# Negative score maxima as matrix rows: a DVE block transpose and eight small transfers in the windows with filler

## The chip, the core and the metric

The kernel runs on one core of a Trainium2 chip. TensorE (PE) multiplies, VectorE (DVE), ScalarE (ACT) and GpSimd (POOL) do the rest, and SyncE (SP) mostly issues DMA transfers. Matmul results land in PSUM, which is used here as eight banks of 128 x 512 floats; all other tiles are in SBUF. The metric is the device time of one execution, in microseconds, as the median of several runs.

## What is computed

A transformer block with adaptive layer norms for 2048 tokens of width 512: 32 attention heads of size 16, then a gated feed-forward layer of width 1792.

```python
mod = (silu(c) @ w_mod).reshape(1, 6, 1, -1)       # sa, ca, ga, sb, cb, gb
h = layernorm(x) * (1 + ca) + sa
q, k, v = split(h @ wqkv)                          # 32 heads of 16
p = softmax(einsum("bhqd,bhkd->bhqk", q, k) * 16 ** -0.5)
x = x + ga * (merge(einsum("bhqk,bhkd->bhqd", p, v)) @ wo)
h = layernorm(x) * (1 + cb) + sb
x = x + gb * ((silu(h @ w_gate) * (h @ w_up)) @ w_down)
```

The softmax needs the maximum of each row of scores, for each head and each query. This change concerns the way in which the negative of that maximum gets into the score matmul.

## The kernel before

All large products are made of float32r matmuls; most operands are split into a high and a low part, and three products of parts are summed.

**Units.** Attention is cut into 32 units (`NU`): a chunk of 512 queries (`ci`, four of them) times a group of four heads (`g`, eight of them). A unit has 16 steps, one for each tile of 128 keys, and each step has four *pairs*, one for each head. A pair (`pair_of`) issues one score matmul for the current step (`score`, L506) with its exponential on ACT (L508), and one matmul of queries by keys for the maxima of a unit that is to come (`max_one`, L479), whose result DVE reduces to one column (L481). The maxima run 20 steps ahead of the scores. The probabilities are multiplied with the values in half-steps (`pv_step`, L521).

**Maxima as rows.** The score matmul has keys on the PSUM partitions and queries along the free axis, so a query's maximum can't be subtracted by a per-partition bias. The operands `qop` (queries) and `kop` (keys) carry two rows more than the 48 of the products: `kop` has ones there, and rows 48 and 49 of `qop` (`KR` = 48; the same at partitions 112 and 113 for the other heads) hold the high and the low part of the negative maximum. The maxima are made with queries on the partitions, so they have to be turned.

**`max_rows(u)`** does that, when the last maximum of a unit has been issued. DVE reduces the four partial maxima to `m`, 128 queries by 16 columns (L486). Five entries are put in the list `side`, from which each following pair takes one: after two empty ones ACT makes `nm`, the negative rounded to float32r (L498) at the third pair, then comes another empty one, and at the fifth pair `rows`: PE multiplies `nm` by the identity (L491), and `m` and `nm` by the negative identity into the same PSUM bank (L492, L493), which gives the high part and the remainder as 16 rows of 256; ACT copies them to `mr` (L495); two transfers on SP's queue put each part into its rows of `qop` (L497). The bank is taken from the turn `bank`, which the score matmuls use too.

**Windows.** The order of all of this is written out by hand. `plain(steps)` runs pairs and half-steps of values alone, with scores on three PSUM banks and maxima on four. `filled(places, work)` runs a window of two steps, eight pairs, and puts between them matmuls of the other layers for an earlier chunk, the *filler* (output projection, gate-up and down products, L719); `places` says how many pieces follow each pair. In such a window scores use two banks (`Turn(4, 5)`), maxima three, and the filler has two of its own. At its end, results of the filler are worked up (`hook`) and up to six half-steps of values run. `end_steps` calls `after(i)` when four pairs are done, and `after` calls `max_rows` in one step of each unit. A gate-up job takes two windows, a down job one. Once the last maxima have been issued, only scores and filler remain in a window, with other places and banks (`ALONE`).

**Queues.** Each engine runs its instructions in the order in which they were issued, and SP's queue too: besides the rows it carries the loads of weights for the filler (`load_gu` at L652, `load_wd` at L657), the softmax denominators (L532, L537, L542) and one half of the loads of `kop` and `qop` (L404). The other half of those loads is on POOL's queue.

Of the kernel before, what the change touches and what calls it, by code (L numbers as in the profile page):

```python
# [9 lines left out]
F32 = mybir.dt.float32  # L10
F32R = mybir.dt.float32r
# [3 lines left out]
ALU = mybir.AluOpType  # L15
AX = mybir.AxisListType
# [3 lines left out]
P = 128  # L20
# [18 lines left out]
KR = 48  # L39
# [62 lines left out]
def block_kernel(ctx, tc, x, wqkv, wo, w_gate, w_up, w_down, c, w_mod, out):  # L102
    nc = tc.nc
# [18 lines left out]
    four, bank, single = Turn(0, 1, 2, 3), Turn(4, 5, 6), Turn(7)  # L122
# [326 lines left out]
    pb = ctx.enter_context(tc.tile_pool(name="pb", bufs=2, reuse_waits="tile"))  # L449
    kop[1] = pb.tile([P, 2, S], F32R, name="kop1", bufs=1)  # L450
    pf = None
    qop, mx, pts, pv, o_, due, res = {}, {}, {}, {}, {}, {}, {}
# [30 lines left out]
    def max_rows(u):  # L483

        m = pb.tile([P, 16], F32, name="m", tag="m")
        nc.vector.tensor_reduce(m, mx.pop(u).rearrange("p b s t f -> p (b s t) f"), op=ALU.max, axis=AX.X)  # L486
        nm = pb.tile([P, 16], F32R, name="nm", tag="nm")

        def rows():
            pr = bank("pr")[0:16, 0:2 * P]  # L490
            nc.tensor.matmul(pr[:, 0:P], nm.bitcast(F32), ident, start=True, stop=True)  # L491
            nc.tensor.matmul(pr[:, P:2 * P], m, minus, start=True, stop=False)  # L492
            nc.tensor.matmul(pr[:, P:2 * P], nm.bitcast(F32), minus, start=False, stop=True)  # L493
            mr = pb.tile([16, 2, P], F32R, name="mr", tag="mr", bufs=1)
            nc.scalar.copy(mr, pr.rearrange("p (r q) -> p r q", r=2))  # L495
            for r in range(2):
                nc.sync.dma_start(qop[u][KR + r:KR + r + 65:64].bitcast(F32), mr[:, r, :].bitcast(F32))  # L497
        side.extend([lambda: None, lambda: None, lambda: nc.scalar.mul(nm, m, -1.0), lambda: None, rows])  # L498

    def score(i, h):  # L500
        u, kt = divmod(i, 16)
        rows = slice(64 * (h % 2), 64 * (h % 2) + KR + 2)
        p_ = pb.tile([P, CW], F32, name="pt_", tag="pt", bufs=PTS)
        pts.setdefault(i, {})[h] = p_
        sp = bank("st_")
        nc.tensor.matmul(sp, kop[u % 3][rows, h // 2, kt * P:(kt + 1) * P], qop[u][rows, h // 2, :],  # L506
                         start=True, stop=True)
        nc.scalar.activation(p_, sp, AF.Exp, scale=SCALE)  # L508
# [51 lines left out]
    def tile_gu():  # L560
        return pf.tile([P, 4, NK, P], F32R, name="wgu", tag="wgu", bufs=2)
# [4 lines left out]
    def tile_mid():  # L566
        return pf.tile([P, 2, CW], F32R, name="mid", tag="mid", bufs=3)
# [4 lines left out]
    def as_wo(w):  # L572
        return w.rearrange("p (b k) x c -> p b k (x c)", b=2)

    def split_weights():

        def raw(src, k):
            t = tile_mid().bitcast(F32)
            nc.gpsimd.dma_start(t.rearrange("p e c -> p (e c)").rearrange("p (k c) -> p k c", k=k), src)
            return t  # L580

        def parts(hi, lo, t):
            nc.gpsimd.tensor_copy(hi, t)
            nc.gpsimd.tensor_sub(lo, t, hi.bitcast(F32))

        def store(dst, w):
            nc.gpsimd.dma_start(dst, w.bitcast(F32))

        def cols(m):
            return slice(m * FG * P, (m + 1) * FG * P)  # L590

        srcs = [(wod[:, 2 * k:2 * k + 2, :], 2) for k in range(NK // 2)]
        for m in range(NF // FG):
            srcs += [(wgd[:, :, cols(m)], NK), (wud[:, :, cols(m)], NK), (wdd[:, m * FG:(m + 1) * FG, :], FG)]
        ahead = [raw(*srcs.pop(0)) for _ in range(2)]
        yield

        def following():
            if srcs:
                ahead.append(raw(*srcs.pop(0)))  # L600
            return ahead.pop(0)

        for k in range(NK // 2):
            t = following()
            nc.gpsimd.tensor_mul(t, t, ga_bc[:, None, :].to_broadcast([P, 2, D]))
            w = tile_gu()
            parts(as_wo(w)[:, 0], as_wo(w)[:, 1], t)
            store(wo_dr[k], as_wo(w))
            yield
        for m in range(NF // FG):  # L610
            ws = [tile_gu() for _ in range(FG)]
            for e in range(2):
                t = following()
                src = t.rearrange("p e c -> p (e c)").rearrange("p (k f c) -> p f k c", k=NK, f=FG)
                for f in range(FG):
                    parts(ws[f][:, 2 * e], ws[f][:, 2 * e + 1], src[:, f])
                    if e:
                        store(gu_dr[m * FG + f], ws[f])
                yield
            t = following()  # L620
            nc.gpsimd.tensor_mul(t, t, gb_bc[:, None, :].to_broadcast([P, FG, D]))
            w = tile_wd()
            parts(w[:, 0], w[:, 1], t)
            store(wd_dr[m], w)
            yield

    class Chunk:
# [42 lines left out]
        def rows(self, t):  # L670
            return self.nt[t // 2][:, t % 2, :]
# [139 lines left out]
    side = []  # L811
# [53 lines left out]
    at(UG - 2, lambda: chunks[0].load_wo())  # L865

    weights2 = split_weights()

    def after(i):
        nonlocal pf  # L870
        for f in due.pop(i, []):
            f()
        j = i + LEAD
        if j % 16 == 15 and j < n:
            max_rows(j // 16)
        if i == -2:
            run(late)
            sm.finish()
            es_a0.close()
            pf = ctx.enter_context(tc.tile_pool(name="pf", bufs=1, side="right", reuse_waits="tile"))  # L880
            kop[2] = pf.tile([P, 2, S], F32R, name="kop2")
            ones_rows(2)
            load_k(2)
            load_q(2)
        if 0 <= i < UG and i % 16 in (3, 5, 8):
            next(weights2, None)
# [48 lines left out]

    def plain(steps, tails=()):

        nonlocal four, bank
        assert steps % WIN == 0 and done % 4 == 0
        four, bank = Turn(0, 1, 2, 3), Turn(4, 5, 6)  # L940
        for w in range(4 * steps // WIN):
            for _ in range(WIN):
                pair_of()
            if w >= 4 * steps // WIN - len(tails):
                tails[w - 4 * steps // WIN](four())
            pvs((HALVES[(w - 2) % 4] if done > 8 else 0) + (w == 4 * steps // WIN - 1), True)
            end_steps()

    def filled(places, work):

        nonlocal four, bank
        four, bank = three, Turn(4, 5)
        if done >= 4 * n - 4 * (LEAD - 1):
            places, bank = ALONE.get(places, places), Turn(4, 5, 0, 1, 5, 0, 4, 1)
        for r in range(len(places)):
            pair_of()
            take(work, places[r])
            if r % 4 == 3:
                end_steps()
        hook()  # L960
        pvs(6, False)
# [105 lines left out]
```

## Time and profile before

| what | value |
|---|---|
| median of 3 runs | 1880.32 us (1879.69 to 1880.54) |
| span of the profiled execution, first to last instruction | 1875.6 us |
| mean granted TensorE clock in it | 0.999 |
| POOL busy | 415.3 us |
| TensorE weight loads, beside the matmuls | 1160.4 us |
| L506 score matmuls, mean of one | 427 ns, 2048 of them |
| L481 reductions of maxima on DVE, mean of one | 682 ns, 2048 of them |
| L497 transfers of rows, each | 8.0 KB, 64 of them |

The span is the time from the first to the last instruction of the profiled execution; the time of a run also holds what lies before and after them. A row of a group gives the line in the code, the engine, the operation, the result and its operands with their shapes, the count, then busy time and the mean of one, and behind the second bar the time for which the engine stood idle just before such instructions, with what ended it. A row of the timeline gives start, length, engine and line, and in brackets the idle time before it. Matmuls overlap in time, so their lengths add up to more than the engine's busy time.

### The profile page before, as it was taken

Reading aid. Unit: us, or ns where it says so; the run is one execution under the profiler, and the core shown is the slowest. Engines: PE = TensorE matmul, PEld = TensorE weight load, DVE = VectorE, ACT = ScalarE, POOL = GpSimd, SP = SyncE. Lnnn points to the kernel's source line nnn. Section 1 sums busy time; section 2 is a strip of 40 time slices with the busy share of each in tenths; the row PEclk is TensorE's granted clock in tenths of the full one; section 3 lists DMA queues with packets and bytes.
Section 4 is the critical chain, followed back from the end, with each engine's and each line's share of the span. In section 5 each row is a group of like instructions: output and inputs, shape, how many; then the busy total and the mean of one; then the engine's idle time right before and its main releaser. Section 6 shows DMA issues by size and latency. Waiting matters only on the chain.

```text
span 1875.6 us, 41002 instructions
## 1 busy us (share of the span) xinstructions
PE 1846.7 (98%) x16996; PEld 1160.4 (62%) x16996; DVE 1541.8 (82%) x2558; ACT 1252.4 (67%) x2406; POOL 415.3 (22%) x498
## 2 busy tenths in 40 slices
PE   7999999999999999999999999999999999999999
PEld 5766444444455766666555667666554566667887
DVE  5548999999999888888999888889999988831643
ACT  4221888888887766777777776677878877674211
POOL 3000454456323211111133111111123011030200
PEclk9999999999999999999999999999999999999999
DMA  8855677766843534554454454453643446243642
GB/s 286 292 198 142 174 183 178 201 167 190 211 86 78 145 102 124 144 124 90 107 124 116 108 127 131 121 122 78 159 86 56 108 92 156 86 159 119 249 180 110
DMA packets 78854, 267.62 MB, mean 143 GB/s; under 512 B 17364, under 2 KB 22484, under 8 KB 57988
## 3 DMA queue, kind: packets, MB, share of 16 engines
q1 hardware_dynamic: 59820, 180.10, 33.0%
q0 software_dynamic: 18160, 84.10, 19.0%
q8 instruction: 133, 2.18, 0.5%
q10 hardware_dynamic: 688, 0.80, 0.1%
q14 instruction: 53, 0.43, 0.1%
HBM read 201.85 MB, written 62.13 MB: 141 GB/s over the span
## 4 chain that ended last, share of the span: by engine, by line
PE 95%; DVE 2%; ACT 2%; DMA 0%; issue 0%; SPq 0%; ACTq 0%; DVEq 0%
PE bank L521 26%; PE bank L506 22%; PE bank L719 19%; PE bank L479 10%; PE bank L729 7%; PE bank L209 7%; DVE mx L481 1%; PE bank L762 1%; PE bank L491 1%; PE bank L162 0%; PE bank L703 0%; DMA wm_ab<-in_w_mod 0%; DVE stt L745 0%; PE bank L279 0%; PE bank L493 0%; PE bank L492 0%
## 5 line engine op out<-in xcount | busy, mean ns | idle before, releaser
L481 DVE TENSOR_REDUCE mx<-bank 128x1 f32<-128x512 f32 x2048 | 1286.5, 682 | 119.5 <-PE bank L479 72.4
L479 PE MATMUL bank<-kop,qop 48*128 48x512 f32 x2048 | 748.0, 432 | 3.6 <-DVE mx L481 3.4
L506 PE MATMUL bank<-qop,kop 50*128 50x512 f32 x2048 | 742.1, 427 | 4.6 <-ACT pt__20499 L508 0.5
L506 PEld LDWEIGHTS bank<-qop,kop 50*128 50x128 f32 x2048 | 347.0, 184 | 305.6 <-issue 63.3
L479 PEld LDWEIGHTS bank<-kop,qop 48*128 48x128 f32 x2048 | 343.9, 184 | 30.7 <-DVE mx L481 14.4
L719 PE MATMUL bank<-act,wgu 64*128 64x512 f32 x1872 | 297.9, 392 | 0.0
L719 PEld LDWEIGHTS bank<-act,wgu 64*128 64x128 f32 x1872 | 188.4, 187 | 30.9 <-DVE m L779 0.3
L548 POOL TENSOR_TENSOR on<-o,rb 128x512 f32<-128x512 f32 x31 | 39.7, 1282 | 442.9 <-DMA rb<-d_dr 304.0
L719 PE MATMUL bank<-wd,mid 64*128 64x512 f32 x912 | 136.5, 397 | 0.0
L781 POOL CAST mid<-m 128x512 fp32r<-128x512 f32 x40 | 24.3, 609 | 430.1 <-PE bank L479 165.5
L719 PEld LDWEIGHTS bank<-wd,mid 64*128 64x128 f32 x912 | 93.3, 185 | 12.0 <-issue 0.8
L209 PE MATMUL bank<-hT,wqs 128*128 128x512 f32 x384 | 95.7, 399 | 2.1 <-DVE prt L369 0.8
L209 PEld LDWEIGHTS bank<-hT,wqs 128*128 128x128 f32 x384 | 70.3, 188 | 24.3 <-issue 6.1
L777 DVE SCALAR_TENSOR_TENSOR q<-th,bank 128x512 f32<-128x512 f32 x56 | 37.7, 673 | 57.4 <-ACT th L773 57.2
L773 ACT ACTIVATE th<-bank 128x512 f32<-128x512 f32 x56 | 33.2, 593 | 58.3 <-PE bank L729 57.9
L793 DVE TENSOR_TENSOR x<-bank,x 128x512 f32<-128x512 f32 x84 | 53.8, 684 | 20.4 <-PE bank L506 20.2
L369 DVE TENSOR_TENSOR prt<-bank,prt 128x512 fp32r<-128x512 f32 x32 | 22.0, 688 | 46.5 <-ACT prt L367 46.5
L367 ACT CAST prt<-bank 128x512 fp32r<-128x512 f32 x32 | 18.8, 587 | 60.2 <-PE bank L209 46.9
L779 DVE TENSOR_TENSOR m<-bank,q 128x512 f32<-128x512 f32 x56 | 38.7, 691 | 21.2 <-PE bank L729 19.1
L729 PE MATMUL bank<-wd,mid 128*128 128x512 f32 x216 | 52.1, 394 | 0.4 <-DVE mid L782 0.3
L782 POOL TENSOR_TENSOR mid<-m,mid 128x512 fp32r<-128x512 f32 x40 | 51.6, 1291 | 3.3
L719 PE MATMUL bank<-wgu,act 64*128 64x512 f32 x288 | 47.7, 394 | 0.1
(6282 smaller groups left out, 5155.0 us busy)
## 6 DMA issues: line engine op xcount, KB each, us to landing
wgu<-gu_dr SPq DMA_DIRECT2D x48, 1024.0 KB
wd<-wd_dr SPq DMA_DIRECT2D x28, 1024.0 KB
kop<-kd SPq DMA_DIRECT2D x33, 768.0 KB
kop<-kd POOLq DMA_DIRECT2D x29, 768.0 KB, 8.5
gu_dr<-wgu POOLq DMA_DIRECT2D x14, 1024.0 KB, 14.1
kd<-prt SPq DMA_DIRECT2D x16, 512.0 KB
qd<-prt SPq DMA_DIRECT2D x16, 512.0 KB
kop<-gu_dr SPq DMA_DIRECT2D x8, 1024.0 KB
```

The costliest lines, as they stand in the source:

```text
L209: nc.tensor.matmul(pt, lhs(a, k), rhs(b, k), start=(n == 0), stop=(n == 3 * nk - 1))
L479: nc.tensor.matmul(pm, qop[u][rows, s, qt * P:(qt + 1) * P], kop[u % 3][rows, s, kc * CW:(kc + 1) * CW], start=True, stop=True)
L481: nc.vector.tensor_reduce(mx[u][:, b, s, qt, kc:kc + 1], pm, op=ALU.max, axis=AX.X)
L506: nc.tensor.matmul(sp, kop[u % 3][rows, h // 2, kt * P:(kt + 1) * P], qop[u][rows, h // 2, :], start=True, stop=True)
L521: nc.tensor.matmul(pv[u][32 * h:32 * h + 32, cols], v_flat[:, e0:e0 + 32], p_[h][:, cols], start=(kt == 0 and half == 0), stop=(kt == 15), ...
L548: mul.tensor_mul(on, o, rb)
L719: nc.tensor.matmul(outs[e], lhs(e, a, k)[rows], rhs(b, k)[rows], start=(ph == 0 and j == 0), stop=(j == z and (ph == 1 or trade is not None)),
L729: nc.tensor.matmul(outs[e], lhs(e, a, k), rhs(b, k), start=(j == 0), stop=(j == z))
L777: nc.vector.scalar_tensor_tensor(q, th, 1.0, outs[0], op0=ALU.add, op1=ALU.mult)
L779: nc.vector.tensor_mul(m32, outs[1], q)
L782: (nc.gpsimd if slow else nc.vector).tensor_sub(mid[:, 1, :], m32, mid[:, 0, :].bitcast(F32))
L793: nc.vector.tensor_add(ch.x2[:, t, :], outs[e], ch.x2[:, t, :])
```

## The change

`max_turned(u)` is added beside `max_rows(u)`, and a flag `beside` chooses between them: `filled` sets it and `plain` clears it. In `max_turned` the tile `parts` holds, for each of 128 queries, 16 high parts and 16 low parts. At the second following pair ACT writes the high parts; at the fourth DVE writes the low parts (`m` times -1, less the high part) and transposes `parts` in four blocks of 32 x 32 into `turned`; at the fifth eight transfers on SP's queue bring the rows of the blocks to `qop`, 16 partitions by 32 floats each, one for each part and each block of 32 queries. The three PE products with the identities, the PSUM bank and the ACT copy are not issued in these units.

```diff
--- before.py
+++ after.py
@@ -497,6 +497,26 @@
                 nc.sync.dma_start(qop[u][KR + r:KR + r + 65:64].bitcast(F32), mr[:, r, :].bitcast(F32))
         side.extend([lambda: None, lambda: None, lambda: nc.scalar.mul(nm, m, -1.0), lambda: None, rows])
 
+    def max_turned(u):
+
+        m = pb.tile([P, 16], F32, name="m", tag="m")
+        nc.vector.tensor_reduce(m, mx.pop(u).rearrange("p b s t f -> p (b s t) f"), op=ALU.max, axis=AX.X)
+        parts = pb.tile([P, 2, 16], F32R, name="parts", tag="parts", bufs=1)
+        turned = pb.tile([P, 32], F32, name="turned", tag="turned", bufs=1)
+
+        def blocks():
+            nc.vector.scalar_tensor_tensor(parts[:, 1], m, -1.0, parts[:, 0].bitcast(F32), op0=ALU.mult,
+                                           op1=ALU.subtract)
+            nc.vector.transpose(turned, parts.rearrange("p r j -> p (r j)").bitcast(F32))
+
+        def rows():
+            for r in range(2):
+                for p in range(4):
+                    dst = qop[u][KR + r:KR + r + 65:64].bitcast(F32).rearrange("b s (t q) -> b (s t) q", t=4)
+                    j = 32 * p + 16 * r
+                    nc.sync.dma_start(dst[:, :, 32 * p:32 * p + 32], turned[j:j + 16])
+        side.extend([lambda: None, lambda: nc.scalar.mul(parts[:, 0], m, -1.0), lambda: None, blocks, rows])
+
     def score(i, h):
         u, kt = divmod(i, 16)
         rows = slice(64 * (h % 2), 64 * (h % 2) + KR + 2)
@@ -865,6 +885,7 @@
     at(UG - 2, lambda: chunks[0].load_wo())
 
     weights2 = split_weights()
+    beside = False
 
     def after(i):
         nonlocal pf
@@ -872,7 +893,7 @@
             f()
         j = i + LEAD
         if j % 16 == 15 and j < n:
-            max_rows(j // 16)
+            (max_turned if beside else max_rows)(j // 16)
         if i == -2:
             run(late)
             sm.finish()
@@ -935,7 +956,8 @@
 
     def plain(steps, tails=()):
 
-        nonlocal four, bank
+        nonlocal four, bank, beside
+        beside = False
         assert steps % WIN == 0 and done % 4 == 0
         four, bank = Turn(0, 1, 2, 3), Turn(4, 5, 6)
         for w in range(4 * steps // WIN):
@@ -948,7 +970,8 @@
 
     def filled(places, work):
 
-        nonlocal four, bank
+        nonlocal four, bank, beside
+        beside = True
         four, bank = three, Turn(4, 5)
         if done >= 4 * n - 4 * (LEAD - 1):
             places, bank = ALONE.get(places, places), Turn(4, 5, 0, 1, 5, 0, 4, 1)
```

## The prediction

> **What bounds the kernel now.** I read the page first (busy time, chain of waits, costliest groups), then the order of time around one of the places that the change touches.
>
> ```profile
> span 1875.6 us, 41002 instructions
> ...
> PE 1846.7 (98%) x16996; PEld 1160.4 (62%) x16996; DVE 1541.8 (82%) x2558; ACT 1252.4 (67%) x2406; POOL 415.3 (22%) x498
> ...
> PE 95%; DVE 2%; ACT 2%; DMA 0%; issue 0%; SPq 0%; ACTq 0%; DVEq 0%
> ...
> L479 PE MATMUL bank<-kop,qop 48*128 48x512 f32 x2048 | 748.0, 432 | 3.6 <-DVE mx L481 3.4
> L506 PE MATMUL bank<-qop,kop 50*128 50x512 f32 x2048 | 742.1, 427 | 4.6 <-ACT pt__20499 L508 0.5
> ```
>
> PE is busy 98% of the span and makes up 95% of the chain that ended last. Over the whole run it stood idle 3.6 us before the maximum matmuls (L479) and 4.6 us before the score matmuls (L506). So work taken off PE should come off the end, as long as nothing new holds PE up.
>
> The change acts only where the flag `beside` is set as a unit's maxima fall due: counting windows in `plain` and `filled` by the constants, that is in 15 of 32 units (11 to 16, 19 to 24, 29 to 31). Unit 11 in order of time on PE (start, length, what):
>
> ```profile
> 629.43 0.50 PE L506 MATMUL bank<-qop,kop 50*128 50x512 f32 x1
> 629.43 0.50 PE L479 MATMUL bank<-kop,qop 48*128 48x512 f32 x1
> 629.86 0.39 PE L491 MATMUL bank<-ident,nm 128*16 128x128 f32 x2
> 630.09 0.38 PE L492 MATMUL bank<-minus,m 128*16 128x128 f32 x2
> 630.31 0.38 PE L493 MATMUL bank<-minus,nm 128*16 128x128 f32 x2
> 630.62 0.49 PE L506 MATMUL bank<-qop,kop 50*128 50x512 f32 x1
> 630.62 0.50 PE L479 MATMUL bank<-kop,qop 48*128 48x512 f32 x1
> ```
>
> The three turning matmuls stand in PE's line from 629.86 to 630.62, 0.76 us in which no score or filler runs.
>
> **The change part by part.**
>
> *Removed from PE.* The bare price is 15 x 0.76 = 11.4 us. A better yardstick is in the trace itself: a window of `filled` (two steps, eight pairs, filler, six value half-steps) that holds a turn, beside one of the same kind that holds none. Each row runs from the start of a window's first score matmul to that of the next window; the second column is its length, then busy time by engine.
>
> ```profile
> 629.43:637.13 7.70, 7.70 (x83) 5.21 (x80) 6.31 (x10) 5.53 (x10) 0.00 (x0) 1.00 0.12 28
> 1598.06:1605.76 7.70, 7.70 (x83) 5.19 (x80) 6.33 (x10) 5.53 (x10) 0.00 (x0) 1.00 0.12 26
> 671.31:678.09 6.78, 6.78 (x78) 4.61 (x74) 6.13 (x10) 5.06 (x9) 1.89 (x2) 1.00 0.28 82
> 643.90:650.76 6.86, 6.86 (x76) 4.64 (x73) 6.20 (x10) 5.55 (x10) 0.00 (x0) 1.00 1.00 140
> 740.42:748.30 7.88, 7.88 (x82) 5.39 (x79) 6.63 (x11) 5.10 (x11) 0.00 (x0) 1.00 0.18 35
> 1542.47:1550.34 7.87, 7.87 (x84) 5.35 (x80) 6.65 (x11) 5.12 (x11) 0.00 (x0) 1.00 0.17 36
> 657.60:664.53 6.93, 6.93 (x76) 4.78 (x72) 6.34 (x11) 4.65 (x10) 0.00 (x0) 1.00 0.17 35
> 699.41:706.43 7.02, 7.02 (x76) 4.80 (x72) 6.42 (x11) 5.11 (x11) 0.00 (x0) 1.00 1.01 145
> 901.06:909.30 8.24, 7.85 (x83) 5.19 (x80) 6.55 (x12) 5.04 (x12) 1.08 (x2) 1.00 0.16 65
> 1314.03:1322.29 8.26, 7.87 (x82) 5.20 (x78) 6.58 (x12) 5.03 (x12) 1.08 (x2) 1.00 0.17 67
> 1653.34:1660.63 7.29, 7.24 (x74) 4.55 (x71) 1.22 (x2) 5.31 (x10) 0.00 (x0) 1.00 0.04 15
> 1674.10:1679.94 5.84, 5.84 (x68) 4.21 (x65) 0.00 (x0) 4.35 (x8) 0.00 (x0) 1.00 0.81 331
> ```
>
> Gate-up windows: rows 1 and 2 are the first and last of nine with a turn, 7.70; rows 3 and 4 have none, 6.78 and 6.86, mean 6.82. Difference 0.88, times nine 7.9 us. Down windows: rows 5 and 6 are the first and last of three with a turn, 7.875 on the mean; rows 7 and 8 without, mean 6.975; 0.90 times three, 2.7 us. Units 16 and 24 (rows 9 and 10, 8.25) sit in the last down window of a chunk, where PE also stood 0.39 us (8.24 less 7.85 busy) in front of the turn for a PSUM bank; 8.25 less 6.975 is 1.275, twice 2.55 us. Unit 31 (row 11) falls where no maxima are left: 7.29 against 5.84 of the next kind, 1.45 us. Sum 14.6 us. It already holds the turn's slot in the rotation of two banks, and that the pair after it could not follow the pair before it directly.
>
> *Removed from ACT.* One copy of 16x256 per unit. ACT is not on the chain in these windows (5.5 of 7.7 us busy), so this counts for nothing by itself.
>
> *Moved on ACT.* The multiplication by -1 is issued one pair earlier. It must still end before DVE reaches the new subtraction, and the maxima `m` must be there when ACT gets to it. DVE (first and third fence line) and ACT (second) around unit 11 and, last two, unit 13:
>
> ```profile
> 625.99 2.53 DVE L481 TENSOR_REDUCE mx<-bank 128x1 f32<-128x512 f32 x4
> ...
> 627.69 0.21 ACT L498 ACTIVATE nm<-m 128x16 fp32r<-128x16 f32 x1
> ...
> 630.00 0.69 DVE L481 TENSOR_REDUCE mx<-bank 128x1 f32<-128x512 f32 x1 [1.49 <-PE bank L506]
> ...
> 739.50 1.27 DVE L481 TENSOR_REDUCE mx<-bank 128x1 f32<-128x512 f32 x2
> 741.00 0.69 DVE L481 TENSOR_REDUCE mx<-bank 128x1 f32<-128x512 f32 x1 [0.22 <-PE bank L506]
> ```
>
> `m` is made just ahead of the four reductions that begin at 625.99; an activation of one pair earlier than 627.69 finds it done. On DVE the subtraction comes behind those four, at 628.52; even at its old place the product is ready at 627.90. Neither engine waits.
>
> *Added to DVE.* Two small operations, a subtraction of 128x16 and a transpose of 128x32. The trace has no transpose. Nearest rows:
>
> ```profile
> L684 DVE SCALAR_TENSOR_TENSOR rs<-rs,rs x3: 161/161/163, 1742.1 to 1743.3; 128x4 f32<-128x4 f32 x3
> ...
> L486 DVE TENSOR_REDUCE m<-mx x32: 200/220/221, 176.8 to 1650.0; 128x16 f32<-128x64 f32 x32
> ...
> L506 PEldq EVENT_SEMAPHORE  x33: 51/51/51, 186.9 to 1660.9; - x33
> ```
>
> From below 2 x 0.16 = 0.32 us; from above, with a transpose three times the reduction of twice its elements, 0.16 + 0.66 = 0.82. I take 0.40, since both shapes lie between the two rows. They run while PE does value matmuls: in unit 11 DVE is idle for 1.49 us just there, so they cost nothing. In a down window the idle time is only 0.22 us, so the next reduction starts about 0.2 us late; three PSUM banks turn for the maxima, so PE is held only if that delay passes the time to the fourth pair. I count nothing. Without this cover it would be 15 x 0.40 = 6.0 us, at the upper price 12.3.
>
> *Added waits on PE.* The first score matmul of a unit must wait for eight transfers in place of two, each with its own semaphore. The last row above shows one extra 51 ns waiting instruction per unit on PE's sequencer; a pair of semaphores fits in one, so up to three more: 15 x 3 x 0.051 = 2.3 us if all of it is exposed, nothing if the sequencer is ahead. I take a quarter, 0.6.
>
> *Added to SP's queue.* Eight issues for two. SP's issues, the first score of unit 11 on PE (the 16th pair after its maxima fell due), and the bytes moved between 687.2 and 689.0 us, when unit 12's two rows are the only transfers:
>
> ```profile
> 631.12 1.13 SPq L497 DMA_DIRECT2D qop<-mr  x2
> ...
> 664.93 0.34 SPq L537 DMA_DIRECT2D d_dr<-dn  x1
> ...
> 667.41 0.56 SPq L542 DMA_DIRECT2D rb<-d_dr  x1
> ...
> 639.83 0.39 PE L506 MATMUL bank<-qop,kop 50*128 50x512 f32 x1
> ...
> GB/s 0 0 0 0 0 0 0 0 0 0 0 23 46 23 34 46 12 0 0 0 0 0 0 0 23 46 23 46 46 0 0 0 0 0 0 0 0 0 0 0
> ```
>
> An issue takes 1.13 / 2 = 0.57 us. A small SP transfer, from its issue to the issue of the load that reads what it wrote, takes 667.41 - 664.93 = 2.48 us. The two bursts in the last row are 13 slices of 45 ns apart, 0.58 us: transfers follow each other at the pace of issue. So in unit 11 the transpose is done at 628.52 + 0.40 = 628.92, the eighth transfer is issued 7 x 0.57 = 4.0 us later, at 632.9, and lands at about 635.4, 4.4 us before 639.83. Behind the rows on SP stand the loads of weights (wgu, wd) and of the denominators; the rows start 2.2 us sooner than at 631.12 and take 4.5 instead of 1.1, so those are held by 1.2 us at most, and they fetch a window or more ahead. Nothing counted.
>
> **Sum.** 14.6 - 0.6 = 14.0 us off the span of 1875.6; the median of the runs, 1880.32, lies 4.7 us over that span, which the change leaves alone. Forecast 1866.3 us.
>
> **The rivals.**
>
> *B: only the bare matmul time comes back.* The wait for the bank or the broken pairing reappears behind the next pair. For it: scores have only two banks here. Against: the windows without a turn run the same pairs on the same banks and are the short ones. Then 15 x 0.76 = 11.4, so 1868.9 us.
>
> *C: DVE becomes the limit.* The two operations are fully exposed: 1866.3 + 6.0 = 1872.3. For it: DVE is busy 6.3 to 6.6 us of windows that shrink to 6.9. Against: L479 waited 3.4 us for DVE in the whole run. The Trainium skill (VectorE: DVE Perf Modes, Rules for kernel authors) speaks for this rival: chained DVE operations pay a drain each, and their number is what to keep low. The 161 ns of a 128x4 operation agrees that the price is mostly fixed.
>
> *D: the rows come late, and it gets slower.* If the eight transfers ran one behind another at 2.48 us, the last would land at 628.9 + 19.8 = 648.7, and PE, in order, would stand at the unit's first score for 8.9 us: 15 x 8.9 = 133 less 14.6, so about 1999 us. It begins to cost above (639.83 - 628.92) / 8 = 1.36 us per transfer and outweighs the gain from about 1.49. Against it: the bursts 0.58 us apart. The Trainium skill (DMA: Bandwidth & Descriptors, Specifications) gives 512 B as the smallest piece at full rate, below it a read-modify-write; the pieces fall from 512 to 128 bytes here, and no run yet shows such pieces.
>
> *E: nothing gained.* The flag is clear when the maxima fall due, or SP's delay makes filler wait for its weights by as much as is saved: 1880.3.
>
> **How the numbers follow.** Forecast 66%, B 13%, C 11%, E 4%, D 6%. A change of under 0.2% (3.8 us) can't be told from none. Forecast, B and C are all faster by more: 0.90; same 0.04; slower 0.06. The range starts at 1864: the whole 14.6 with no new cost is 1865.7, with the shorter control windows alone (6.78, 6.93) 0.6 us less, and 1 us is left for what a less loaded ACT may give. It ends at 1872.5, just past C.
>
> **What would show it.** L491 to L493 with 34 records each in place of 64; the nine gate-up windows at about 6.8 us, the down windows at 7.0, unit 31's at 5.9; two new DVE groups of 15, under 0.82 us together, with PE idle before L479 on DVE still near 3.4 us; eight SP issues of 0.57 us per unit; no idle time of L506 behind the transfer of `turned`. The forecast is wrong if the windows keep 7.3 us or more, if L506 waits for a DMA, or if PE's idle time before L479 grows by microseconds.

## The result, and the profile after

| what | before | changed |
|---|---|---|
| first measurement, median of 4 runs each | 1880.43 us (1879.69 to 1884.03) | 1863.21 us (1862.89 to 1864.45) |
| span of the profiled execution | 1875.6 us | 1861.0 us |
| all runs of the two kernels, this measurement and two repeats | four medians from 1879.49 to 1880.43 (53 runs) | median 1864.5 us (14 runs, 1862.03 to 1869.98) |

The ratio of the first measurement is 0.9909 [0.9894, 0.9924], a gain of 17.2 us. That is 3.1 us more than forecast, and 0.8 us below the lower end of the range. Two repeats gave 0.9929 and 0.9919; the mean of the three ratios puts the gain at 15.2 us. By their medians the two repeats gained 13.5 us each.

The changed kernel's page: span, busy time of each engine, the chain that ended last, and the groups of maximum and score matmuls (behind the bar busy time and mean ns of one, then idle time before them).

```profile
span 1861.0 us, 41049 instructions
...
PE 1832.9 (98%) x16906; PEld 1152.3 (62%) x16906; DVE 1542.6 (83%) x2588; ACT 1245.7 (67%) x2391; POOL 414.9 (22%) x498
...
PE 93%; DVE 2%; ACT 2%; DMA 2%; SPq 0%; issue 0%; ACTq 0%; DVEq 0%
...
L479 PE MATMUL bank<-kop,qop 48*128 48x512 f32 x2048 | 745.0, 431 | 3.2 <-DVE mx L481 1.9
L526 PE MATMUL bank<-qop,kop 50*128 50x512 f32 x2048 | 738.1, 427 | 4.6 <-ACT pt__20559 L528 0.5
```

PE is busy 13.8 us less, almost the whole 14.6 by which the span fell, and still 98% of it. The idle time before the maximum matmuls (now 3.2 us) and before the score matmuls (4.6 us; their line is now L526) has not grown: nothing new holds PE up there. The DMA share of the chain, 2% now and 0% before, has five transfers of the last unit in it, 16.7 us; they come back below, under the end of the kernel.

The windows of the changed kernel that answer to those shown of before: from the first score matmul of a window to that of the next, with its length, busy time of PE, weight loads, DVE, ACT and POOL (instructions in brackets), the granted clock, the DMA share and GB/s.

```profile
628.59:635.36 6.77, 6.77 (x76) 4.61 (x73) 6.13 (x10) 5.05 (x9) 0.00 (x0) 1.00 0.13 29
1584.14:1590.94 6.80, 6.80 (x76) 4.78 (x73) 6.15 (x10) 5.06 (x9) 0.00 (x0) 1.00 0.14 25
737.76:744.69 6.93, 6.93 (x76) 4.77 (x73) 6.62 (x13) 4.64 (x10) 0.00 (x0) 1.00 0.12 18
1529.40:1536.37 6.97, 6.97 (x77) 4.94 (x74) 6.62 (x13) 4.60 (x10) 0.00 (x0) 1.00 0.12 22
895.52:902.51 6.99, 6.99 (x76) 5.02 (x72) 6.69 (x14) 4.68 (x11) 1.08 (x2) 1.00 0.20 80
1302.51:1309.50 6.99, 6.99 (x76) 5.01 (x72) 6.63 (x14) 4.67 (x11) 1.08 (x2) 1.00 0.19 76
1638.53:1644.40 5.87, 5.87 (x68) 4.16 (x64) 1.20 (x2) 4.82 (x9) 0.00 (x0) 1.00 0.10 35
```

In each row PE's busy time equals the length: the windows are full, and have the length of those that never held a turn. The 0.39 us that PE stood before the turn of units 16 and 24 is gone too. Summed over all 15 windows, the difference from before is 15.1 us (0.93 on the mean in twelve of them, 1.25 and 1.27 in units 16 and 24, 1.42 in unit 31). In the profiles of the two repeats (e2 and e10) the same windows give 15.1 us again, and in that of the kernel before (e1) 0.0: what differs from one execution to another lies outside them.

The new operations in the changed kernel's trace, by line: the shortest, median and longest duration in ns, the first and last start, the shape.

```profile
L508 DVE SCALAR_TENSOR_TENSOR parts<-m,parts x15: 161/166/177, 627.6 to 1636.3; 128x16 fp32r<-128x16 f32 x15
...
L510 DVE STREAM_TRANSPOSE turned<-parts x15: 211/211/214, 627.8 to 1636.7; 128x32 f32<-128x32 f32 x15
...
L526 PEldq EVENT_SEMAPHORE  x78: 51/51/51, 185.8 to 1645.0; - x78
...
L491 PE MATMUL bank<-ident,nm x34: 272/278/284, 176.4 to 1475.7; 128*16 128x128 f32 x34
```

L491 has the 34 records that show the flag set in 15 units. The two DVE operations take 0.38 us, and PE's sequencer has 45 waiting instructions of 51 ns more than before, three for each unit. Around unit 11 the changed kernel's timeline (start, length, engine) shows DVE and SP:

```profile
626.39 1.29 DVE L481 TENSOR_REDUCE mx<-bank 128x1 f32<-128x512 f32 x2
627.59 0.17 DVE L508 SCALAR_TENSOR_TENSOR parts<-m,parts 128x16 fp32r<-128x16 f32 x1
627.79 0.21 DVE L510 STREAM_TRANSPOSE turned<-parts 128x32 f32<-128x32 f32 x1
629.16 1.29 DVE L481 TENSOR_REDUCE mx<-bank 128x1 f32<-128x512 f32 x2 [1.16 <-PE bank L479]
...
628.03 4.37 SPq L517 DMA_DIRECT2D qop<-turned  x8
...
633.38 0.33 SPq L672 DMA_DIRECT2D wgu<-gu_dr  x1
```

After the two operations DVE still waits 1.16 us for PE. The eight issues take 4.37 us; the last of the 128-byte packets was recorded at 633.13, and the unit's first score matmul began at 638.05, 4.9 us later. In the down windows that margin is 3.6 us, in units 16 and 24 it is 2.3 us.

### The profile page after: what moved, and what is told of

The parts are those of the page before. It is cut to its first block, busy times and chain, and to the rows that moved or that the text cites. A ratio compares the mean times of both kernels' runs of the same rounds, so it can differ in the third digit from the quotient of the medians.

```text
span 1861.0 us, 41049 instructions
## 1 busy us (share of the span) xinstructions
PE 1832.9 (98%) x16906; PEld 1152.3 (62%) x16906; DVE 1542.6 (83%) x2588; ACT 1245.7 (67%) x2391; POOL 414.9 (22%) x498
## 4 chain that ended last, share of the span: by engine, by line
PE 93%; DVE 2%; ACT 2%; DMA 2%; SPq 0%; issue 0%; ACTq 0%; DVEq 0%
PE bank L541 27%; PE bank L526 23%; PE bank L739 19%; PE bank L479 10%; PE bank L749 6%; PE bank L209 6%; DVE mx L481 1%; DVE stt L765 1%; PE bank L162 0%; PE bank L723 0%; DMA wm_ab<-in_w_mod 0%; PE bank L491 0%; PE bank L279 0%; DMA kop<-o_dr 0%; DMA rb<-d_dr 0%
## 5 line engine op out<-in xcount | busy, mean ns | idle before, releaser
L526 PE MATMUL bank<-qop,kop 50*128 50x512 f32 x2048 | 738.1, 427 | 4.6 <-ACT pt__20559 L528 0.5
L526 PEld LDWEIGHTS bank<-qop,kop 50*128 50x128 f32 x2048 | 345.6, 184 | 305.5 <-issue 63.1
L479 PEld LDWEIGHTS bank<-kop,qop 48*128 48x128 f32 x2048 | 343.0, 184 | 29.2 <-DVE mx L481 14.5
```

Source lines behind the costliest of these rows:

```text
L479: nc.tensor.matmul(pm, qop[u][rows, s, qt * P:(qt + 1) * P], kop[u % 3][rows, s, kc * CW:(kc + 1) * CW], start=True, stop=True)
```

## The experiments

**How far one execution differs from another.** The kernel before and the changed kernel were run again unchanged: the one as e1, the other as e2 and, on another chip, as e10.

> The kernel before, unchanged, for the spans of its timed runs. The windows with a turn account for 15.1 us between the two profiles, while the medians of the runs stand 17.2 us apart and the profiled spans 14.6 us (1875.6 to 1861.0). Theory S (the profiled execution of before was a short one): its timed runs have spans near 1878.5 us, that is 1.9 us under their times, as the changed kernel's runs do, and a second profile is longer than 1875.6 in the opening or in the tail, not in the windows. Rival O (the time outside the span differs): spans near 1875.6 with times near 1880.4, that is 4.7 us outside.

> The changed kernel, unchanged, for a closer ratio on the same chip as e1. Theory S: median between 1862.5 and 1864.5 us, ratio to before 0.990 to 0.992, nine gate-up windows of 6.75 to 6.80 us again. Rival (the first runs of before were slow by chance): the gain shrinks to 15 us, ratio 0.992 or more.

> The changed kernel again, beside e9 and e12 on the same chip, to settle its gain. Theory W (the windows give 15.1 us and the tail takes back 1 to 3 us; the rest of the spread lies in the first 147 steps, 358.0 to 360.4 us in all profiles without a change there): a gain of 12 to 14.5 us, median 1865 to 1868. Rival (the first measurement, 17.2 us, is the true one and something beside the windows gains 2 us more): 1862 to 1864.

Measured: e1 1879.77 us (1876.85 to 1884.29, 11 runs), ratio 1.0003 [0.9994, 1.0011]. e2 1865.97 (1863.09 to 1867.6, 5 runs), ratio 0.9929 [0.9916, 0.9941]. e10 1866.47 (1862.03 to 1869.98, 5 runs), ratio 0.9919 [0.9903, 0.9935]. In each execution the time is 1.7 to 1.9 us over the span, in both kernels (1879.06 for a span of 1877.3 in e1, 1862.89 for 1861.0). The rest of the differences lies inside the span, as theory S of e1 had it. In e2 the rival came true (a ratio of 0.992 or more), in e10 theory W (a gain of 12 to 14.5 us). The slowest of e10, with a span of 1868.1, was profiled; its timeline around 403 us, in unit 5, where the change issues nothing:

```profile
403.07 0.25 DVE L556 RECIPROCAL dn<-dn 128x16 f32<-128x16 f32 x1 [1.34 <-DMA dn<-o]
...
403.93 0.49 PE L479 MATMUL bank<-kop,qop 48*128 48x512 f32 x1 [0.89 <-DVE mx L481]
```

and the windows of the same stretch in e10, in the columns used above:

```profile
403.00:404.00 1.00, 0.11 (x3) 0.08 (x2) 0.93 (x3) 0.91 (x2) 0.00 (x0) 1.00 1.01 188
...
405.00:406.00 1.00, 1.00 (x13) 0.53 (x16) 1.00 (x3) 0.09 (x1) 0.00 (x0) 0.54 0.96 182
406.00:407.00 1.00, 1.00 (x10) 0.27 (x4) 0.85 (x2) 0.00 (x0) 0.00 (x0) 0.50 0.96 236
407.00:408.00 1.00, 1.00 (x6) 0.56 (x6) 0.40 (x1) 0.43 (x1) 0.00 (x0) 0.50 1.11 260
408.00:409.00 1.00, 1.00 (x14) 0.44 (x16) 1.00 (x3) 1.00 (x3) 0.00 (x0) 0.76 0.96 367
```

A denominator came late from DMA, DVE waited 1.34 us for it, the maxima behind it waited, and PE stood for 0.89 us. Then the granted clock fell to one half for 3.41 us (the seventh column), and the unit took 42.08 us where the first profile of the changed kernel has 39.26. At 582.6 us the clock fell once more, for 6.83 us; there PE had stood no longer than 0.21 us in the 10 us ahead of it. In the profiled execution of before the clock shows no such stretch ahead of the kernel's end. In e1 there is one of 3.41 us at 193 us, and the 147 steps from the first score on take 359.63 us there in place of 357.98. Just ahead of it PE had stood for 0.25 and 0.18 us; in the profiled execution of before it stood as long at the same place, 0.25 and 0.19 us, and the clock did not fall. e2 has the same stretch at the same place. Such losses come to nothing in some executions and to several us in others, in both kernels. What decides whether the clock falls is not shown.

**PE's three matmuls and ACT's copy put back**, beside everything that the change added; their result is not used (e3; e11 is the same without the last two lines).

```diff
         def rows():
+            pr = bank("pr")[0:16, 0:2 * P]
+            nc.tensor.matmul(pr[:, 0:P], parts[:, 0].bitcast(F32), ident, start=True, stop=True)
+            nc.tensor.matmul(pr[:, P:2 * P], m, minus, start=True, stop=False)
+            nc.tensor.matmul(pr[:, P:2 * P], parts[:, 0].bitcast(F32), minus, start=False, stop=True)
+            mr = pb.tile([16, 2, P], F32R, name="mr", tag="mr", bufs=1)
+            nc.scalar.copy(mr, pr.rearrange("p (r q) -> p r q", r=2))
```

> The turned rows as in the changed kernel, and beside them the three PE products, their PSUM bank and the ACT copy again, whose result nobody reads. Theory (the gain is PE's slot and the bank, and DVE's two operations and the eight transfers cost nothing): the 15 windows go back to 7.70, 7.9 and 8.25 us, and the time to before's, ratio to before 0.999 to 1.001. Rival (part of the gain came from elsewhere, from the shorter way over SP or the earlier product on ACT): the time stays 2 us or more below before. Rival (DVE's additions or the transfers cost something that the gain hid): 2 us or more above before.

> The turned rows as in the changed kernel, with the three PE products and their PSUM bank put back but no ACT copy behind them. Theory (PE's own time and the place in the line make the 0.93 us, the copy none): the gate-up windows take 7.70 us again. Rival (the copy holds the bank and with it the next score): 7.5 us or less.

Measured: e3 1880.99 us (1878.21 to 1885.52, 10 runs), ratio 1.0007 [0.9996, 1.0018]; e11 one run, 1876.6, with a span of 1874.8. The windows of units 11 and 13, of e3 and then of e11:

```profile
630.83:638.54 7.71, 7.71 (x82) 5.44 (x79) 6.28 (x10) 5.53 (x10) 0.00 (x0) 1.00 0.12 23
741.84:749.72 7.88, 7.88 (x82) 5.39 (x79) 6.81 (x13) 5.10 (x11) 0.00 (x0) 1.00 0.18 40
```

```profile
628.55:636.26 7.71, 7.71 (x83) 5.45 (x79) 6.28 (x10) 5.17 (x9) 0.00 (x0) 1.00 0.12 21
739.61:747.46 7.85, 7.85 (x82) 5.39 (x78) 6.81 (x13) 4.72 (x10) 0.00 (x0) 1.00 0.17 33
```

With the transpose, the eight transfers and their waits still in place, the windows are back at the 7.70 and 7.88 us of before, and the whole gain is gone. So it came from PE's three matmuls with their bank, and the new path costs nothing there that can be measured. Without the copy ACT is busy 0.36 us less and the windows stay: the copy contributes nothing. What the bank alone contributes was not tried.

**The DVE operations, four times over.**

```diff
+            for _ in range(4):
                 nc.vector.scalar_tensor_tensor(parts[:, 1], m, -1.0, ...)
                 nc.vector.transpose(turned, parts.rearrange("p r j -> p (r j)").bitcast(F32))
```

> Only the windows with filler turn, as in the changed kernel, but the subtraction and the transpose are issued four times over: 3 x 0.38 = 1.1 us more on DVE in each of the 15 units. Theory (DVE has room in these windows, 1.49 us of idle time in a gate-up window while PE multiplies values): the gate-up windows stay at 6.8 us, the down windows lengthen by 0.5 us at most, in all under 3 us over the changed kernel, near 1867 us. Rival C (DVE is the limit there): 15 x 1.1 = 17 us more, back to 1880 us or above.

Measured: 1868.7 us (1867.6 to 1870.38, 4 runs), ratio 0.9942 [0.9928, 0.9957]: near the 1867 of the theory, far from the 1880 of rival C. The windows of units 11, 13 and 16 in e5:

```profile
629.28:636.04 6.76, 6.76 (x76) 4.57 (x73) 6.61 (x14) 5.05 (x9) 0.00 (x0) 1.00 0.10 15
738.49:746.15 7.66, 7.60 (x76) 4.83 (x72) 7.42 (x19) 4.74 (x10) 0.00 (x0) 1.00 0.02 4
896.99:905.01 8.02, 7.49 (x77) 5.22 (x73) 7.50 (x20) 4.67 (x11) 0.80 (x2) 1.00 0.16 63
```

The 1.14 us of DVE time that was added (three times 0.38) disappears in the gate-up window, which stays at 6.76. In the down windows it costs 0.73, in those of units 16 and 24 1.03: 3 x 0.73 + 2 x 1.03 = 4.2 us, which is the rise from the pooled 1864.5. DVE's cover differs from window to window, and only five of the fifteen are near their limit.

**The rows sent six pairs later.**

```diff
-        side.extend([..., lambda: None, blocks, rows])
+        side.extend([..., lambda: None, blocks] + [lambda: None] * 6 + [rows])
```

> The eight transfers are issued six pairs later, some 5 us. In the trace of the changed kernel the last bytes land 4.9 us before the unit's first score in a gate-up window (633.13 to 638.05), 3.6 us in a down window, 2.3 us in units 16 and 24. Theory (rows that come late hold PE, one for one): PE waits 1 to 3.5 us a unit at the first score, with transfers of `turned` named as the cause, 20 to 30 us more in all, near 1890 us. Rival (the room is larger, since the sequencer and the queues are ahead): the time of the changed kernel, 1863 to 1867 us.

Measured: 1886.6 us (1872.91 to 1897.02, 10 runs), ratio 1.0028 [1.0000, 1.0056]. The profiled execution was one of the fastest, with a span of 1874.0. Its table of waits (idle engine, tile and line, what ended it, then us, times, longest):

```profile
PE bank L527 <- DMA qop<-turned: 4.6, 3, 1.8
...
PE bank L740 <- DMA wgu<-gu_dr: 2.7, 2, 1.6
```

The first row is the prediction's rival D, in which the rows come late, now real; the second is one that the prediction priced at nothing: filler waiting for weights that stand behind the rows on SP's queue. The theory had a wait in each of the 15 units; in this execution the rows held PE in three of them (13, 21 and 29, whose turns fall in down windows). The longest wait, 1.8 us, cost more than itself: the window that holds it took 10.31 us in place of 6.77, with the clock at one half for 3.41 us. The other two, 1.35 and 1.49 us, had no such fall behind them. The median lies 10.8 us above the profiled execution, and no trace shows what the slower runs waited for. The margin of 2.3 to 4.9 us is what keeps the change on the good side.

**The new path in all 32 units**, also in those with nothing but plain steps around it (e4); and the same with the low part left out, so that DVE has a fill in place of the subtraction (e7).

```diff
-            (max_turned if beside else max_rows)(j // 16)
+            max_turned(j // 16)
```

```diff
-            nc.vector.scalar_tensor_tensor(parts[:, 1], m, -1.0, parts[:, 0].bitcast(F32), ...)
+            nc.vector.memset(parts[:, 1].bitcast(F32), 0.0)
```

> The block transpose in all 32 units, also in the windows without filler, where PE is busy 100% and DVE 99% of the time in the trace of before. Theory D (DVE sets the pace there, with four reductions of 0.61 us in a step of 2.44 us): the 17 further units gain nothing on PE and pay 0.17 + 0.21 us on DVE, 17 x 0.38 = 6.4 us, so about 1869.5 us. Rival P (PE sets the pace there too): they gain 0.83 us each, 14 us, so about 1849 us. Both at once, each taking a part: between the two, near 1863.

> As e4, the block transpose in all 32 units, but the subtraction, which reads two tiles, is replaced by a fill with zeros, which reads none: the low part of the negative maximum is left out. In e4 that subtraction took 0.76 to 1.60 us in units 2 to 8, each time until POOL's instruction ended, and 0.16 us elsewhere. Theory (DVE waited for POOL there, and PE lost its clock behind it): the fill takes 0.2 us or less in every unit, the first 147 steps go back from 392 us to 358 to 362 us, and the time to 1863 to 1870 us. Rival (the rows come late in windows without filler, whatever the subtraction takes): units 1 to 8 stay 4 us longer than before, and the time over 1890 us.

Measured: e4 1923.12 us (1899.76 to 1926.85, 4 runs), ratio 1.0209 [1.0159, 1.0259]; e7 1885.97 (1880.71 to 1893.97) in the eight runs that its ratio counts, 1.0036 [1.0022, 1.0051], and 1916.21 and 1918.56 in two more. e4 is far above all three times that were named for it, e7 between the two. The profiled execution of e4 is its fastest; for the 22 to 27 us by which the other three are longer there is no trace. The timeline of e4 in unit 3:

```profile
309.48 2.37 POOL L604 TENSOR_TENSOR wd<-mid,wd 128x1024 fp32r<-128x1024 f32 x1
...
310.37 1.51 DVE L508 SCALAR_TENSOR_TENSOR parts<-m,parts 128x16 fp32r<-128x16 f32 x1
311.92 0.21 DVE L510 STREAM_TRANSPOSE turned<-parts 128x32 f32<-128x32 f32 x1
...
312.76 0.50 PE L479 MATMUL bank<-kop,qop 48*128 48x512 f32 x1 [1.40 <-DVE mx L481]
```

The subtraction, 0.17 us elsewhere, takes 1.51 us and ends at 311.88, 0.03 us after POOL's instruction (309.48 + 2.37 = 311.85). In units 2 to 8, where POOL prepares weights, it took 0.36 us (unit 5) to 1.60 us and ended each time as POOL's instruction did, and so it did in unit 17 (0.41 us). The transpose behind it took its 0.21 us beside running POOL instructions too. The Trainium skill (SBUF — State Buffer, SBUF: two separate sides) says that a DVE operation with two SBUF inputs and a GpSimd operation that reads SBUF lock each other out for a whole instruction. The trace agrees in these eight units: the operation with two inputs waits, the one with one input doesn't. It does not agree everywhere: in units 10, 18 and 26 the subtraction took 0.16 us inside a running POOL operation with an input in SBUF (a TENSOR_SCALAR from `x` to `mid`), by the records at least. e7 shows the fill, with no input, in the view by line; the waits of e7 stand below it in a fence of their own:

```profile
L508 DVE MEMSET parts<- x32: 72/72/72, 176.3 to 1663.5; 128x16 f32 x32
```

```profile
PE bank L525 <- DMA qop<-turned: 8.1, 6, 2.0
...
PE bank L525 <- issue: 4.6, 2, 4.5
```

The fill takes 72 ns in every unit, so the wait for POOL is gone. From the first score to the 148th step, in which the changed kernel takes 358.19 us, e4 took 392.06 and e7 379.00, each in one execution: of the 34 us 13 went with that wait, and about 21 stayed. Those are rows that land late for the score matmuls. In 15 of the 17 units without filler PE stood before the first score, for 0.16 to 4.49 us, and began it 0.4 to 1.6 us after the last of the unit's 128-byte packets. The table of waits names the rows for six of these stands, 8.1 us. The 4.5 us that it puts to "issue" are unit 2's: the last packet was recorded at 273.19 and the score began at 274.15. The half clock comes on top, 23.9 us of it in these steps, though not behind each stand: those of 1.79 and 1.47 us in front of units 3 and 6 had none. Both suspected costs were there, and neither alone explains e4.

**Six more units whose maxima fall due in plain steps, without POOL's weight splitting beside them**, and with half of their transfers on POOL's queue to bring them sooner.

```diff
-            (max_turned if beside else max_rows)(j // 16)
+            (max_turned if beside or j // 16 in (17, 18, 25, 26, 27, 28) else max_rows)(j // 16)
...
-                    nc.sync.dma_start(dst[:, :, 32 * p:32 * p + 32], turned[j:j + 16])
+                    eng = nc.gpsimd if r and u in (17, 18, 25, 26, 27, 28) else nc.sync
+                    eng.dma_start(dst[:, :, 32 * p:32 * p + 32], turned[j:j + 16])
```

> The changed kernel, and beside it the block transpose in the later units without filler (17, 18, 25 to 28), where POOL is mostly idle, with the low parts' four transfers on POOL's queue, so that the rows land some 2 us sooner than in e4. Theory (there PE sets the pace as well, and only the late rows ate the gain in e4): 0.3 to 0.8 us a unit, 2 to 5 us below the changed kernel. Rival (DVE sets the pace there): the same time as the changed kernel, or up to 2 us more.

Measured: 1890.04 us (1886.6 to 1893.9), ratio 1.0062 [1.0045, 1.0079]: slower, and neither the theory nor the rival is decided by it, since the rows came later and not sooner. The timeline of e8 around one such unit, SP and then POOL:

```profile
941.08 2.19 SPq L518 DMA_DIRECT2D qop<-turned  x4
...
947.70 1.26 POOL L689 TENSOR_TENSOR act<-act,act 128x512 fp32r<-128x512 f32 x1
948.90 2.25 POOL L518 DMA_DIRECT2D qop<-turned  x4
```

SP issued its four at 941.08, POOL its four at 948.90, 7.8 us later, since the products of the filler's results stood ahead of them on POOL. PE waited up to 6.2 us for those rows, and the clock was at one half for 10.24 us. A queue is only as soon as the engine that carries it.

**Seven more units, on SP alone and two pairs sooner.**

```diff
-        side.extend([lambda: None, lambda: nc.scalar.mul(parts[:, 0], m, -1.0), lambda: None, blocks, rows])
+        mul = lambda: nc.scalar.mul(parts[:, 0], m, -1.0)
+        side.extend([lambda: None, mul, lambda: None, blocks, rows] if beside else [mul, blocks, rows])
...
-            (max_turned if beside else max_rows)(j // 16)
+            (max_turned if beside or j // 16 in (10, 17, 18, 25, 26, 27, 28) else max_rows)(j // 16)
```

> The changed kernel and the block transpose also in seven units without filler in which POOL is mostly idle (10, 17, 18, 25 to 28), there with product, subtraction and transfers at the first three pairs in place of the second, fourth and fifth, so that the rows land some 1.2 us sooner than in e4 and e7, where PE waited 0.2 to 1.5 us for them. Theory (only the late rows ate the gain there): 0.3 to 0.8 us a unit, 2 to 5 us below e10. Rival (DVE sets the pace there too and its 0.38 us are paid in full): the same as e10 within 1 us, or above.

Measured: 1866.19 us (1864.09 to 1871.56), ratio 0.9927 [0.9913, 0.9940], beside 1866.47 of the changed kernel on the same chip: no difference that the spread of the runs would show. No score waits for rows now, so it is the pace that gives little. Steps 155 to 167, around unit 10's maxima, take 33.51 us in place of 33.75. Steps 267 to 275, around unit 17's, and the window behind them, of the changed kernel and then of e12:

```profile
932.97:953.65 20.68, 20.43 (x216) 9.50 (x212) 20.59 (x36) 18.18 (x37) 10.26 (x13) 1.00 0.58 156
953.65:960.46 6.81, 6.80 (x72) 4.89 (x72) 5.71 (x9) 4.56 (x8) 0.00 (x0) 1.00 1.05 149
```

```profile
935.11:955.48 20.37, 20.32 (x211) 9.39 (x207) 20.34 (x37) 17.58 (x36) 10.39 (x14) 1.00 0.58 152
955.48:962.61 7.13, 7.13 (x76) 5.21 (x72) 6.01 (x10) 4.77 (x9) 0.00 (x0) 1.00 1.01 144
```

What the plain steps save there, 0.31 us, the window behind them gives back. Over all seven units about 1 us comes off, where the theory had 2 to 5, and in the profiled executions the end took more than that back (168.74 us; 166.71 in e10). Plain steps give back most of what PE saves, as the rival had it. That DVE is their limit is argued and not shown: in the plain steps of e12 DVE is busy 20.34 and PE 20.32 of 20.37 us. PE's time is worth its length, and a little more, in the windows with filler alone.

**The end of the kernel.** From the last step to the end the profiled execution of before took 164.61 us, that of the changed kernel 166.29. One suspicion was the number of ACT instructions ahead of it, which the change lowers; e9 puts them back, two of one element for each unit.

```diff
+        spare = pb.tile([1, 1], F32, name="spare", tag="spare", bufs=1)
...
         def rows():
+            for _ in range(2):
+                nc.scalar.copy(spare, parts[0:1, 0, 0:1].bitcast(F32))
```

> The changed kernel and, in each of the 15 units, two copies of one element on ACT that nobody reads, 30 instructions more. From the last step on, the six profiles with before's number of ACT instructions or 32 units turned take 164.6 to 164.9 us, the five with 15 or 21 units turned and no copy put back 165.5 to 167.7, since a DMA that ACT issues in the last unit's chain goes out 0.8 to 2 us late, and the trace shows no wait for it. Theory I (ACT's instructions shifted, so that a fetch of instructions falls into that chain): with the 30 back, the tail is 164.6 to 165.0 us. Rival (another cause, that goes with the gain itself): the tail stays at 165.5 us or more.

Measured: 1863.42 us (1862.87 to 1863.68), ratio 0.9908 [0.9894, 0.9921]; the end took 165.81 us. The suspicion is not borne out, and e11, which has the changed kernel's ACT count, has an end of 164.94. Part of the loss can be seen in two issues on ACT's queue in the last unit, before and then after:

```profile
1717.55 0.35 ACTq L537 DMA_DIRECT2D d_dr<-dn  x1
...
1719.03 0.56 ACTq L542 DMA_DIRECT2D rb<-d_dr  x1
```

```profile
1701.29 0.35 ACTq L557 DMA_DIRECT2D d_dr<-dn  x1
...
1703.66 0.56 ACTq L562 DMA_DIRECT2D rb<-d_dr  x1
```

The second issue, which waits for the first transfer, comes 2.37 us after it in place of 1.48. The DMA queues of the changed kernel between the two issues (packets, MB, share of the 16 DMA engines):

```profile
q10 hardware_dynamic: 144, 0.01, 3.7%
q8 instruction: 1, 0.02, 2.7%
```

In the profile of before q10 has the same 144 packets between the two issues, and q8 has none. A packet of q8, 16384 bytes, comes once in some 250 records of PE and its weight loads all through the traces, so it is taken here for a fetch of PE's instructions. The change takes 90 matmuls and 90 weight loads out, and so moves the places at which these fetches fall. In the 14 profiles the place goes with the end:

| first q8 packet between 5 and 18 us after the start of the last step | profiles | the end, us |
|---|---|---|
| none | before, e1, e4, e7 | 164.6 |
| at 15.4 to 15.6 us | e3, e11 | 164.9 |
| at 6.5 to 6.7 us, beside the first of the two issues | changed kernel, e2, e10, e5, e6, e9 | 165.5 to 167.7 |
| at 14.4 to 14.5 us | e8, e12 | 167.3, 168.7 |

In the third row the second issue comes 2.3 to 2.8 us after the first, in all the others 1.5 to 1.6; in the last row a later transfer of the same chain is late. So a fetch of instructions does fall into the chain, as theory I had it, but with PE's instructions and not ACT's, and e9's copies left PE's where they were. This rests on 14 profiles; no run moved PE's instructions alone to test it.

## Why the prediction was right in kind and 3.1 us off

- **The terms of the sum: right, slightly small.** The windows were to give 14.6 us and gave 15.1; the controls of before were taken at a mean of 6.82, and the windows with a turn came down to 6.75 to 6.80, the length of the shorter control (6.78). That the turn costs more than its 0.76 us of matmuls, against rival B, is shown by e3: with the matmuls back, all of the 0.94 us of unit 11's window returns.
- **The waits on PE: priced at 0.6, worth nothing.** The three extra waiting instructions in each unit are there. They stand at the unit's first score, and the two steps around the fifteen first scores take as long as before, to 0.1 us in sum.
- **DVE: 0.40 predicted, 0.38 measured, hidden as predicted.** e5 bounds the cover: another 1.14 us is free in a gate-up window, and costs 0.73 to 1.03 in the others. Rival C was false at this size, and begins to be true at a few times it.
- **The rows: 4.4 us ahead of the score predicted, 4.9 measured** in unit 11, with eight issues in 4.37 us. Rival D did not happen, and e6 made it happen in three units by moving them six pairs; behind one of the three waits the halved clock came on top, which the prediction's price for that rival, a sum of waits, leaves out.
- **ACT: nothing predicted, nothing found** (e11). In one of the 15 units DVE waited 1.0 us for ACT's product, against "Neither engine waits", and that unit's window kept its 5.87 us.
- **The end of the kernel: not foreseen.** It gave back 1.7 us in the profiled execution, 0.9 in e2's and 2.1 in e10's; the sum had no term for it. The opening, up to the first score, happened to be 1.1 us shorter (188.03 for 189.10; e1 has 188.83 with the code of before). So 15.1 + 1.1 - 1.7 = 14.5, of the 14.6 by which the span fell.
- **The step that failed:** "the median of the runs, 1880.32, lies 4.7 us over that span, which the change leaves alone". Only 1.8 of the 4.7 us lie outside the span. The profiled execution of before therefore took about 1877.4 us, below all three runs shown, and it lacked 2.9 us that these had inside their spans. Of those three runs there is no trace; in e1 and e10 such differences are in good part stretches at half clock, which come in some executions and not in others. The forecast carried the 2.9 us over as fixed, and the first four runs of the changed kernel (spans 1861.0 to 1862.7) were, by their spans, without most of them. From the profiled execution's own time the same sum gives 1875.6 + 1.8 - 14.0 = 1863.4. That this is so close to the 1863.21 measured is in part luck: the windows gave 0.5 us more than the sum had, the waits cost 0.6 us less, the opening was 1.1 us shorter by chance, and the end took 1.7 us back.
- **How the 3.1 us split is not settled.** The two repeats, with medians of 1865.97 and 1866.47, lie inside the range and within 0.4 us of the forecast. By them the gain is 13.5 us, which is what the windows' 15.1 less the 0.9 to 2.1 us at the end leave, and all of the 3.1 us is the draw of the first measurement. By the mean of the three ratios the gain is 15.2 us, so that 1.2 us would be gain beyond the 14.0 forecast and the other 1.9 the draw. Nor is it shown whether the draw is made anew in each execution: on one chip the five runs of e10 spread over 8 us, the four of e9 over 0.8.
- **The range.** Its lower end had 1 us for a lighter ACT, which e11 shows to be nothing, and nothing for the draw.

## What to carry to other kernels

Where PE is full, price a removed PE step by windows of the same kind with and without it, and then see whether the other engines have the slack to let the window shrink: they had it here beside filler, and hardly any in plain steps. A small transfer may take over the work if its row lands before its reader with a margin, and what that margin is worth is the wait and, at times, the clock lost after it. Set the sum against the profiled execution's own time, and give the range the spread of single executions, also where the few runs shown lie close together.

## What the runs showed of the hardware

- The half clock needs little: PE stood 0.89 us in e10 and 1.40 us in e4, and the granted clock then fell to 0.50 in stretches of 3.41 us or a multiple (6.83, 10.24). The Trainium skill (TensorE: Matmul & The Clock Gate, What's actually happening) has the fall after at least one idle window of some 3.4 us. The length agrees; the runs show the fall after far shorter stands. The length of a stand does not decide it: in e10 the clock fell behind one of 0.21 us, in e7 it did not behind one of 1.79 us.
- Eight transfers of 128-byte pieces follow each other at the pace of issue, 0.55 us each, and the last packet was recorded 1.2 us after the last issue began (631.91 to 633.13, unit 11 of the changed kernel). The small pieces brought no queue of their own.
- A DVE transpose of 128x32 floats took 211 ns and ran beside POOL's work unharmed; a subtraction half as large with two inputs waited up to 1.4 us for POOL (e4), though not in each unit in which POOL was busy.
- A packet of 16384 bytes on the queue of instructions, beside a transfer of 8 KB in the chain that ends the kernel, goes with 0.8 to 1.4 us more for that transfer in six of 14 profiles.
